# The last query tile of each value burst behind the query-major scores, and no constant matmul ahead of the burst

## The chip, the core and the metric

The kernel runs on one core of one Trainium2 chip. Its engines work side by side and meet at semaphores: TensorE (PE: matmuls, and PEld: weight loads that overlap them), VectorE (DVE), ScalarE (ACT), GpSimd (POOL), and SyncE (SP), which issues DMAs. Matmuls write to PSUM, from which DVE and ACT read. The metric is the device time of one launch in microseconds (us); less is better.

## What is computed

A block of a network, forward and backward: attention over 2048 tokens with 32 heads of width 18, beside a state-space convolution (S4) with a state of 128 in each of 576 channels, mixed by a gate that depends on the token. The outputs are the block's result and the gradients of eleven of its parameters and of its input. The change lies in the attention part alone, whose forward is:

```
scores = jnp.einsum("bhqd,bhkd->bhqk", q, k) * (Dh ** -0.5)
p = _softmax(scores, axis=-1)
o = jnp.einsum("bhqk,bhkd->bhqd", p, v)
```

Its backward needs, for each head, dv = pT dO, ds = p * (dO vT - row sums), dq = ds k and dk = dsT q. The scores are not kept: p is worked out twice, once with the keys along the partitions (for o and ds) and once with the queries along the partitions (for dv).

## The kernel before

**Stages.** A first stage makes q, k, v and the convolution's parameters; the attention stage follows (about 120 to 2090 us of the profiled span), during which POOL also prepares tables for the convolution; the last stage does the convolution, its gradients and the output projections. Only the attention stage is touched.

**Units and steps.** A unit is four heads and 512 queries; there are 8 x 4 = 32 units. The loop at L1289 runs over steps G; each unit has 32 steps. In a step the first pass works on the unit of the moment and the second pass on work that is 39 steps older (OFF, L1118). All five engines run in the order in which the program is written; nothing is rescheduled.

**One step, in the order in which PE gets it:**
1. *P1*: two matmuls of the first pass, queries times keys, into one tile of the PSUM tag "S" (two buffers of two banks). ACT turns it into PT with an exponential of 128x1024 (L1388).
2. *A burst*, by the slot of the step, which is (G - 38) mod 8. Slots 0 and 1: value gradient accV. Slots 2 and 3: query gradient accQ. Slots 5 and 6: key gradient accK. Slots 4 and 7: transposes (turn_p) or the transposes of a finished output. Every burst writes the one buffer of the PSUM tag "accB", and each is read out by DVE before the next may begin.
3. *P3*: two matmuls of the second pass, query-major scores, into the other tile of "S". ACT turns it into eb (L1393).
4. *P2*: two matmuls, dO times vT, each into its own buffer of the tag "dP" (two buffers). DVE multiplies each with a PT tile into ds (L1398).
5. In slots 1, 2, 5 and 6 four matmuls of the output, accO.

In the trace P1 is ps_P<-QaT_g,KaT_g, P3 is ps_P<-KaT_g,QaT_g and P2 is ps_P<-dOaT,VaT_g; all have line L30, a helper's.

**The value burst.** One key block of 512 keys ("a tile" below means the eight steps of one key block; there are 128) has four query tiles ii = 0 to 3, and the eb tiles of query tile ii come from two steps. dv_half (L1136) runs ii = 0 and 1 in slot 0, and ii = 2 and 3 in slot 1, each with four matmuls. The eb of ii = 3 is finished by ACT in the step just before slot 1. In front of slot 0's half stands the constant matmul, fill (L1131): J_bf times the identity into accB, 512 columns wide; its result is overwritten by the burst's first matmul. NFILL (L955) says how many there are.

**The eviction.** At the end of slot 1's half DVE adds accV to a running sum, dvacc (L1146 to L1151). These closures are collected in evs and run ahead of the ACT and DVE work of the step (L1382):

```
for e_ in evs:
    e_()
for (kind, g, b, i, j, ps) in rows:
```

so that on DVE dvacc stands in front of the two ds of its step.

Of the kernel before, what the change touches and what calls it, by code (L numbers as in the profile page):

```python
# [20 lines left out]
def build(tc, aps, dbg_aps=None, stages=("s1", "attn", "post", "s4", "final")):  # L21
# [40 lines left out]
    with ExitStack() as gctx:  # L62
# [66 lines left out]
        with ExitStack() as ctx:  # L129
# [5 lines left out]
            V, AC, GP = nc.vector, nc.scalar, nc.gpsimd  # L135
# [443 lines left out]
        Q = {}  # L579
# [370 lines left out]
        if "attn" in stages:  # L950
# [3 lines left out]
            DA = HP  # L954
            NFILL = {"V": 1, "Q": 0, "K": 0}  # L955
            with ExitStack() as ctx:
# [131 lines left out]
                def by_pe(p):  # L1088

                    return {NPF: 0, NPF + 1: 1}.get(p, 2)  # L1090
# [45 lines left out]
                def dv_half(g, b, kq, h, acc):  # L1136
                    U = UN[(g, b)]
                    for ii in (2 * h, 2 * h + 1):
                        for j in range(4):
                            mm(acc[HP * j:HP * (j + 1), :], lhsT=U["dOa"][:, ii, j, :], rhs=U["eb"].pop((kq, ii, j)),  # L1140
                               start=(ii == 0), stop=(ii == 3), tile_position=(0, HP * j))

                    def ev():
# [145 lines left out]
                for G in range(NTOT + OFF + 24):  # L1289
# [14 lines left out]
                    if 0 <= G2 < NTOT:  # L1304
                        u2, s2 = divmod(G2, NST)
                        r2 = (units[u2][0], units[u2][1], s2)
                    rows = []
                    if r1:
# [5 lines left out]
                        rows.append(("P1", g, b, i, j0, ps))  # L1314
                    evs = []
                    slot = (G2 + 1) % 8
# [7 lines left out]
                    elif 0 <= m_ < NTOT // 8:  # L1324
                        u_, kq = divmod(m_, NQ)
                        g, b = units[u_]
                        if slot in SLOTS:
                            nm, burst, h = SLOTS[slot]
# [17 lines left out]
                    if r2:  # L1346
# [11 lines left out]
                        for x in range(2):  # L1358
                            j2 = 2 * (1 - par_) + x
                            ps = apsp.tile([P, KB], F32, tag="dP", bufs=2, name="ps_P2")  # L1360
                            row(ps, T["VaT", i2 // TPQ][:, (i2 % TPQ) * P:(i2 % TPQ + 1) * P], U["dOaT"].rearrange("p t q -> p (t q)"), j2)
                            rows.append(("P2", g, b, i2, j2, ps))
                    tail = []
                    if G % 8 in (0, 3, 4, 7) and G >= 3:
# [16 lines left out]

                    for e_ in evs:  # L1382
                        e_()
                    for (kind, g, b, i, j, ps) in rows:
# [9 lines left out]
                        else:  # L1394
# [3 lines left out]
                            nc.vector.tensor_tensor(U["ds"][i][:, j, :], ps, U["PT"][i, j // 2][:, j % 2, :], op=A.mult)  # L1398
                            U["dsn", i] += 1
                            nj = 3 if by_pe(i // 2) >= 2 - i % 2 else 4  # L1400
                            if U["dsn", i] == nj:
# [473 lines left out]
```

## Time and profile before

| what | us |
|---|---|
| runs of the kernel | 2666.23, 2686.29, 2685.02 |
| their median | 2685.02 |
| span of the profiled execution (first to last instruction) | 2673.6 |
| mean granted clock of TensorE in it | 0.968 |

The profile gives of the profiled execution its span alone. A row of a table of groups or of the timeline has: start, length, engine, line, operation, out<-in by the program's names, shapes, count, and in brackets the idle time of the engine before it with what ended that. Matmul lengths are modelled and overlap: four matmuls in different quarters of the array run side by side, so that groups follow each other at 0.32 us although each row says 0.39. ACT's and DVE's rows overlap by the tail of the one before. In a table of windows the columns are the stretch, its length, the busy time of PE, PEld, DVE, ACT and POOL with the number of instructions, the granted clock of TensorE (1.00 is full), the share of the DMA engines and GB/s.

### The profile page before, as it was taken

The page shows a single profiled execution, that of the slowest core. Times are in us where ns is not written, and L with a number is a line of the kernel's source. Part 1 is how long each engine was busy: PE and PEld are TensorE (multiplying, and loading weights), DVE is VectorE, ACT ScalarE, POOL GpSimd, SP SyncE. Part 2 cuts the span into 40 slices and gives each one's busy share as a digit, 9 for nine tenths or more (in the row PEclk, how much of TensorE's full clock was granted, in tenths as well). Part 3 has the DMA queues.
Part 4 walks back from the last instruction along what each step waited for, and adds up shares of the span by engine and source line. Part 5 has one row for each costly group of instructions (what it writes and reads, how often), then busy time and mean ns, then how long its engine had stood idle before and what let it go on. Part 6 is the DMA issues. An engine that isn't in the chain of part 4 may idle for free.

```text
span 2673.6 us, 69952 instructions
## 1 busy us (share of the span) xinstructions
PE 2405.5 (90%) x27411; PEld 1134.6 (42%) x27411; DVE 2294.7 (86%) x4090; ACT 2352.0 (88%) x2744; POOL 1830.1 (68%) x2845
## 2 busy tenths in 40 slices
PE   8999999998889898889898999989988699999999
PEld 4433333333333333333333333333232489998756
DVE  5748999999889999889899999999897499999964
ACT  5589999999999999999999999999996489999321
POOL 0388878888888888888878888887931135555431
PEclk9989999999999999999999999999896699999999
DMA  7747889879979978997898899779668979998996
GB/s 232 202 114 152 150 171 177 162 156 181 169 151 172 185 157 163 173 167 152 165 179 157 157 172 169 154 164 181 134 136 174 224 229 262 260 263 250 269 255 136
DMA packets 1155478, 486.63 MB, mean 182 GB/s; under 512 B 1071062, under 2 KB 1108551, under 8 KB 1152843
## 3 DMA queue, kind: packets, MB, share of 16 engines
q1 hardware_dynamic: 1108346, 339.13, 64.3%
q0 software_dynamic: 44784, 137.52, 19.2%
q10 hardware_dynamic: 2016, 5.51, 0.7%
q8 instruction: 214, 3.51, 0.6%
q14 instruction: 118, 0.96, 0.1%
HBM read 146.27 MB, written 93.80 MB: 90 GB/s over the span
## 4 chain that ended last, share of the span: by engine, by line
ACT 39%; PE 28%; DVE 22%; issue 6%; DMA 3%; POOL 2%; SPq 1%; ACTq 0%; DVEq 0%; POOLq 0%
ACT eb L1393 23%; ACT PT L1388 14%; PE ps_P L30 8%; DVE ds L1398 7%; DVE tz L733 3%; DVE wab L753 3%; PE accV L30 2%; PE ps_dx L30 2%; PE turn_p L1097 2%; DVE tz L736 2%; PE accK L30 2%; DVE HG L738 2%; PE yp L30 2%; DVE Rw L758 1%; DVE dvacc L1151 1%
## 5 line engine op out<-in xcount | busy, mean ns | idle before, releaser
L1398 DVE TENSOR_TENSOR ds<-ps_P,PT 128x512 bf16<-128x512 f32 x2048 | 1312.5, 683 | 127.8 <-PE ps_P L30 87.3
L1393 ACT ACTIVATE eb<-ps_P 128x1024 bf16<-128x1024 f32 x1024 | 1095.7, 1070 | 44.3 <-PE ps_P L30 44.2
L1388 ACT ACTIVATE PT<-ps_P 128x1024 bf16<-128x1024 f32 x1024 | 1099.6, 1075 | 11.0 <-PE ps_P L30 9.5
L30 PE MATMUL ps_P<-dOaT,VaT_g 32*128 32x512 bf16 x2048 | 583.1, 390 | 30.8 <-DVE ds L1398 15.4
L506 POOL TENSOR_TENSOR et<-eG,eT 128x448 f32<-128x448 f32 x576 | 542.9, 963 | 10.7
L30 PE MATMUL ps_P<-QaT_g,KaT_g 32*128 32x512 bf16 x2048 | 404.7, 387 | 126.6 <-ACT PT L1388 122.2
L30 PE MATMUL ps_P<-KaT_g,QaT_g 32*128 32x512 bf16 x2048 | 408.9, 392 | 2.0 <-ACT eb L1393 1.4
L506 POOL TENSOR_TENSOR Eo<-et,et 128x448 bf16<-128x448 f32 x288 | 327.2, 1136 | 20.8
L30 PEld LDWEIGHTS <-KaT_g 32*128 32x128 bf16 x2048 | 147.4, 91 | 456.1 <-issue 438.2
L30 PEld LDWEIGHTS <-QaT_g 32*128 32x128 bf16 x2048 | 115.7, 91 | 288.6 <-issue 266.7
L30 PE MATMUL accV<-eb,dOa 128*32 128x512 bf16 x2048 | 185.6, 396 | 26.8 <-ACT eb L1393 26.5
L30 PE MATMUL accO<-PT,Vtok_g 128*32 128x512 bf16 x2048 | 207.9, 395 | 0.1
L30 PE MATMUL accK<-dsT,Qtok_g 128*32 128x256 bf16 x4096 | 165.3, 283 | 21.3 <-DMA dsT<-ds 19.9
L30 PE MATMUL accQ<-ds,Ktok_g 128*32 128x512 bf16 x2048 | 161.9, 394 | 2.2 <-DVE dvacc L1151 1.9
L30 PEld LDWEIGHTS <-Vtok_g 128*32 128x32 bf16 x2048 | 52.8, 93 | 222.6 <-issue 222.6
L1102 DVE COPY dsT<-turn_p 128x1024 bf16<-128x1024 bf16 (+1 forms) x216 | 139.2, 644 | 3.4 <-PE turn_p L1097 3.4
L1097 PE MATMUL turn_p<-ident_bf,ds 128*128 128x128 bf16 x1664 | 136.2, 225 | 1.4 <-DVE gb L1169 0.8
L672 ACT COPY E1e<-etp 128x1024 bf16<-128x1024 bf16 x132 | 125.4, 1063 | 2.7 <-PE etp L671 2.7
L30 PEld LDWEIGHTS <-Qtok_g 128*32 128x32 bf16 x4096 | 88.6, 97 | 87.8 <-issue 57.9
L506 POOL TENSOR_TENSOR et<-eT 128x32 f32<-128x32 f32 (+3 forms) x288 | 116.2, 424 | 11.4
L1097 PEld LDWEIGHTS <-ds 128*128 128x128 bf16 x1664 | 98.9, 100 | 50.2 <-issue 50.0
L1075 POOL COPY dtk<-gT 128x288 bf16<-128x288 bf16 x96 | 40.9, 426 | 107.6 <-DMA dqkv_d<-dtk 47.2
(295 smaller groups left out, 3731.0 us busy)
## 6 DMA issues: line engine op xcount, KB each, us to landing
E_d<-Eo POOLq DMA_DIRECT2D x144, 256.0 KB, 3.3
E1n<-E_d POOLq DMA_DIRECT2D x30, 1024.0 KB, 6.6
T0w<-Kp_d SPq DMA_DIRECT2D x18, 1024.0 KB
xs<-xb_d POOLq DMA_DIRECT2D x28, 512.0 KB, 9.9
dsT<-ds SPq DMA_TRANSPOSE x512
dqkv_d<-dtk POOLq DMA_DIRECT2D x96, 72.0 KB, 4.3
Md_d<-mst SPq DMA_DIRECT2D x18, 288.0 KB
skw<-Md_d SPq DMA_DIRECT2D x72, 64.0 KB
```

What stands on the lines that cost most here:

```text
L30: return nc.tensor.matmul(out, lhsT=lhsT, rhs=rhs, start=start, stop=stop, **kw)
L506: nc.gpsimd.tensor_tensor(out, a, b, op=op)
L672: copy(E_[:, 4 * q:4 * q + 4], pt_)
L733: nc.vector.tensor_tensor(tz[x], HG[:, :, k - 1].unsqueeze(1).to_broadcast([P, 2, 2, n, CB]), ZZ.unsqueeze(3).to_broadcast([P, 2, 2, n, CB ...
L736: nc.vector.tensor_tensor(tz[x][:, 0], tz[x][:, 0], UVk[:, :, :, k, :], op=A.add)
L738: nc.vector.tensor_tensor(HG[:, :, k], tz[x][:, 0], tz[x][:, 1, ::-1], op=A.add)
L753: nc.vector.tensor_tensor(wab, h_, w_, op=A.mult)
L1097: nc.tensor.transpose(pt_[:, x, qb, :], t_[:, qb * P:(qb + 1) * P], ident_bf)
L1102: (nc.scalar.copy if NTOT <= now[0] < NTOT + OFF else nc.vector.tensor_copy)(o_(), pt_[:, x:x + n])
L1388: nc.scalar.activation(U["PT"][i, j // 2], ps, ACT.Exp)
L1393: nc.scalar.activation(e, ps, ACT.Exp)
L1398: nc.vector.tensor_tensor(U["ds"][i][:, j, :], ps, U["PT"][i, j // 2][:, j % 2, :], op=A.mult)
```

## The change

Three things, all in the attention loop.

First, NFILL["V"] is 0: no constant matmul in front of accV. Second, in slot 1 the four matmuls of query tile 3 are not issued with those of tile 2; they are put in a list, late, and issued behind the step's P3 and P2 rows. Third, in those steps the eviction of accV no longer runs ahead of the ds, but between the first and the second ds of the step.

```diff
-            NFILL = {"V": 1, "Q": 0, "K": 0}
+            NFILL = {"V": 0, "Q": 0, "K": 0}
...
-                    for ii in (2 * h, 2 * h + 1):
+
+                    def stored(ii):
                         for j in range(4):
                             mm(acc[HP * j:HP * (j + 1), :], lhsT=U["dOa"][:, ii, j, :], rhs=U["eb"].pop((kq, ii, j)),
                                start=(ii == 0), stop=(ii == 3), tile_position=(0, HP * j))
+                    stored(2 * h)
+                    if h == 0:
+                        stored(1)
+                    else:
+                        late.append(lambda: stored(3))
...
-                    evs = []
+                    evs, late = [], []
...
                             rows.append(("P2", g, b, i2, j2, ps))
+                    for f in late:
+                        f()
                     tail = []
...
-                    for e_ in evs:
-                        e_()
+                    if not (late and r2):
+                        for e_ in evs:
+                            e_()
...
                             U["dsn", i] += 1
+                            if late and r2 and j % 2 == 0:
+                                for e_ in evs:
+                                    e_()
```

What this does to the order of the instructions, on the two engines that meet there. Names are those of the trace; a row's last number is the shape it writes, and "waits" names the semaphores it has to wait for, by engine. Rows that only repeat, and weight loads, are left out at "...".

PE before, from the P1 of slot 0 to the accQ of slot 2:

```order
L30 MATMUL ps_P_5509<-QaT_g,KaT_g 128x512 [waits Activation_49]
...
L30 MATMUL accV<-ident_bf,J_bf 128x512 [waits DVE_49]
...
L30 MATMUL accV<-eb,dOa_1234 32x512
...
L30 MATMUL ps_P_5522<-KaT_g,QaT_g 128x512 [waits Activation_49]
...
L30 MATMUL ps_P_5540<-QaT_g,KaT_g 128x512 [waits Activation_49]
...
L30 MATMUL accV<-eb,dOa_1234 32x512 [waits Activation_49]
...
L30 MATMUL ps_P_5551<-KaT_g,QaT_g 128x512 [waits PE_49]
...
L30 MATMUL ps_P_5554<-dOaT,VaT_g 128x512 [waits DVE_49]
...
L30 MATMUL accO<-PT,Vtok_g 32x512
...
L30 MATMUL ps_P_5575<-QaT_g,KaT_g 128x512 [waits Activation_49]
...
L30 MATMUL accQ<-ds,Ktok_g 32x512 [waits DVE_49]
```

PE now, the same place:

```order
L30 MATMUL ps_P_5497<-QaT_g,KaT_g 128x512 [waits Activation_49]
...
L30 MATMUL accV<-eb,dOa_1234 32x512 [waits DVE_49]
...
L30 MATMUL ps_P_5509<-KaT_g,QaT_g 128x512 [waits Activation_49]
...
L30 MATMUL ps_P_5527<-QaT_g,KaT_g 128x512 [waits Activation_49]
...
L30 MATMUL accV<-eb,dOa_1234 32x512
...
L30 MATMUL ps_P_5534<-KaT_g,QaT_g 128x512 [waits Activation_49]
...
L30 MATMUL ps_P_5537<-dOaT,VaT_g 128x512 [waits DVE_49]
...
L30 MATMUL accV<-eb,dOa_1234 32x512
...
L30 MATMUL accO<-PT,Vtok_g 32x512
...
L30 MATMUL ps_P_5562<-QaT_g,KaT_g 128x512 [waits Activation_49]
...
L30 MATMUL accQ<-ds,Ktok_g 32x512 [waits DVE_49]
```

The constant matmul is gone, and its wait for DVE (for accB) is now on the first accV. In slot 1 the wait for ACT has moved from the fifth accV to P3 (ps_P_5534), and the last accV stand between P2 and accO. The first accQ waits for DVE in both.

DVE before, slots 0 to 2 (two ds each, the eviction dvacc in slot 1, the dqa of slot 3 as the last row):

```order
L1398 TENSOR_TENSOR ds<-ps_P_5525,PT 128x512 [waits PE_49,Activation_49]
L1398 TENSOR_TENSOR ds<-ps_P_5527,PT 128x512 [waits PE_49]
L1151 TENSOR_TENSOR dvacc<-dvacc,accV 128x512 [waits PE_49]
L1398 TENSOR_TENSOR ds<-ps_P_5554,PT 128x512 [waits DMAHW4_49,PE_49,Activation_49]
L1398 TENSOR_TENSOR ds<-ps_P_5556,PT 128x512 [waits PE_49]
L1398 TENSOR_TENSOR ds<-ps_P_5590,PT 128x512 [waits PE_49,Activation_49]
L1398 TENSOR_TENSOR ds<-ps_P_5592,PT 128x512 [waits PE_49]
L1164 TENSOR_SCALAR dqa<-accQ 128x512 [waits DVE_49,PE_49]
```

DVE now:

```order
L1407 TENSOR_TENSOR ds<-ps_P_5512,PT 128x512 [waits PE_49,Activation_49]
L1407 TENSOR_TENSOR ds<-ps_P_5514,PT 128x512 [waits PE_49]
L1407 TENSOR_TENSOR ds<-ps_P_5537,PT 128x512 [waits DMAHW4_49,PE_49,Activation_49]
L1157 TENSOR_TENSOR dvacc<-dvacc,accV 128x512 [waits PE_49]
L1407 TENSOR_TENSOR ds<-ps_P_5539,PT 128x512
L1407 TENSOR_TENSOR ds<-ps_P_5577,PT 128x512 [waits PE_49,Activation_49]
L1407 TENSOR_TENSOR ds<-ps_P_5579,PT 128x512 [waits PE_49]
L1170 TENSOR_SCALAR dqa<-accQ 128x512 [waits DVE_49,PE_49]
```

dvacc has moved behind the first ds of slot 1, ds<-ps_P_5537, which reads the first P2 of that slot. ACT's, POOL's and SP's own instructions keep their order and number.

## The prediction, made before the changed kernel was run

> **What bounds the kernel now.** I read the page first: busy shares, slices, chain.
>
> ```profile
> PE 2405.5 (90%) x27411; PEld 1134.6 (42%) x27411; DVE 2294.7 (86%) x4090; ACT 2352.0 (88%) x2744; POOL 1830.1 (68%) x2845
> ...
> PEclk9989999999999999999999999999896699999999
> ...
> ACT 39%; PE 28%; DVE 22%; issue 6%; DMA 3%; POOL 2%; SPq 1%; ACTq 0%; DVEq 0%; POOLq 0%
> ```
>
> Over the whole span three engines look alike, so the shares decide nothing. The table of windows, asked for the attention stage alone, does: ACT is busy in 1807.93 of 1821.00 us.
>
> ```profile
> 180.00:2001.00 1821.00, 1640.65 (x17627) 570.29 (x17626) 1634.33 (x2692) 1807.93 (x1962) 1512.70 (x2462) 0.99 0.85 163
> ```
>
> Only 13.1 us of idle ACT are left there, and PE and DVE each have over 180 us. The stage lasts as long as ACT's row of exponentials, and any edit is worth what it does to that row. Next the timeline of ACT over one tile, from slot 0 (PT at 1016.16) to slot 2.
>
> ```profile
> 1016.16 1.17 ACT L1388 ACTIVATE PT<-ps_P 128x1024 bf16<-128x1024 f32 x1
> 1017.16 1.08 ACT L1393 ACTIVATE eb<-ps_P 128x1024 bf16<-128x1024 f32 x1
> 1018.08 1.07 ACT L1388 ACTIVATE PT<-ps_P 128x1024 bf16<-128x1024 f32 x1
> 1019.11 1.02 ACT L1393 ACTIVATE eb<-ps_P 128x1024 bf16<-128x1024 f32 x1
> 1020.03 1.02 ACT L1388 ACTIVATE PT<-ps_P 128x1024 bf16<-128x1024 f32 x1
> 1020.94 1.03 ACT L1393 ACTIVATE eb<-ps_P 128x1024 bf16<-128x1024 f32 x1
> ```
>
> Neighbours overlap, so starts mislead; the ends (start plus length) are 1017.33, 1018.24, 1019.15, 1020.13, 1021.05, 1021.97. They are 0.91 to 0.92 apart, but 0.98 at the eb of slot 1. That is what the value burst costs ACT: 0.07 us a tile. Slot 0, where the constant matmul stands, costs it nothing: 0.91. PE and DVE over the same stretch:
>
> ```profile
> 1015.86 0.39 PE L30 MATMUL accV<-ident_bf,J_bf 128*128 128x512 bf16 x1
> 1016.18 0.61 PE L30 MATMUL accV<-eb,dOa 128*32 128x512 bf16 x8
> 1016.73 0.39 PE L30 MATMUL ps_P<-KaT_g,QaT_g 32*128 32x512 bf16 x2
> 1016.74 0.39 PE L30 MATMUL ps_P<-dOaT,VaT_g 32*128 32x512 bf16 x2
> ...
> 1018.29 0.40 PE L30 MATMUL accV<-eb,dOa 128*32 128x512 bf16 x4 [0.20 <-ACT eb L1393]
> 1018.62 0.39 PE L30 MATMUL ps_P<-KaT_g,QaT_g 32*128 32x512 bf16 x2
> 1018.63 0.39 PE L30 MATMUL ps_P<-dOaT,VaT_g 32*128 32x512 bf16 x2
> ...
> 1019.28 0.39 PE L30 MATMUL ps_P<-QaT_g,KaT_g 32*128 32x512 bf16 x2
> 1019.60 0.61 PE L30 MATMUL accQ<-ds,Ktok_g 128*32 128x512 bf16 x8
> 1020.19 0.39 PE L30 MATMUL ps_P<-KaT_g,QaT_g 32*128 32x512 bf16 x2
> ```
> ```profile
> 1017.26 1.29 DVE L1398 TENSOR_TENSOR ds<-ps_P,PT 128x512 bf16<-128x512 f32 x2 [0.66 <-PE ps_P L30]
> 1018.74 0.69 DVE L1151 TENSOR_TENSOR dvacc<-dvacc,accV 128x512 f32<-128x512 f32 x1 [0.18 <-PE accV L30]
> 1019.34 2.67 DVE L1398 TENSOR_TENSOR ds<-ps_P,PT 128x512 bf16<-128x512 f32 x4
> ```
>
> In slot 1 the last four accV matmuls wait for the eb that ends at 1018.24, start 0.05 later, and the P3 rows that feed the next eb stand behind them. The list of waits counts 125 such places:
>
> ```profile
> PE accV L30 <- ACT eb L1393: 26.5, 125, 0.8
> ```
>
> **The change, part by part.**
>
> *The move, its gain.* P3 needs only the buffer that the same eb releases, so it starts at 1018.29 in place of 1018.62. The eb needs it 0.49 earlier than its own start (1018.62 to 1019.11) and is then no longer late. Gain: 0.07 x 125 = 8 us; the other end is 0.
>
> *The move, the new wait.* accB has one buffer. The query burst of slot 2 may write it when DVE has read accV out, and DVE, in its new order, does that behind the first ds of slot 1, which waits for the first P2 row, which stands behind P3. Worked out with the latencies above:
> - P3 at 1018.29, P2 at 1018.30.
> - From P2 to its ds is 0.52 (1016.74 to 1017.26): first ds at 1018.82. DVE is free by then (its ds of slot 0 end at 1018.55).
> - DVE starts its next read 0.61 later (two ds take 1.29, one 0.68): dvacc at 1019.43, 0.69 long, ends 1020.12. It ended at 1019.43 before. Its own input, the moved matmuls behind P2, is long there: P2 at 1018.30 plus 0.32 a group, plus 0.45 from accV to dvacc, is 1019.07.
> - accQ 0.05 later: 1020.17, where it was 1019.60.
> - Eight such matmuls hold PE for 0.55 (1016.18 to 1016.73): P3 of slot 2 at 1020.72.
> - eb 0.49 later at 1021.21, 1.02 long: ends 1022.23. It ended at 1021.97.
>
> So the tile is 0.26 us longer with the gain of slot 1 already in it: without the wait eb would end at 1021.90. Times 125: **+32 us**. Lower end: P3 to eb took 0.43 once (1016.73 to 1017.16), which makes 0.20 and +25. Upper end: if everything that accQ is late, 0.57, reached ACT, less the 0.07, +62; but accQ had 0.2 of slack, so I take the worked-out value, nearer the lower end. Queued behind the waiting accQ on PE are P3, P2 and accO of slot 2; behind dvacc on DVE is the second ds, which ends about 0.1 later than before, and DVE has idle time in the next slots for that. In the order SP and POOL have the same 852 and the same POOL instructions; no DMA is added or moved past another. The transposed loads that read a finished dvacc are issued two steps later and find it done.
>
> *The constant matmul, its gain.* 128 instructions of 0.32 (1015.86 to 1016.18). At most 41 us if PE were the bound; ACT's ends in slot 0 are 0.91 apart, so 0: the matmul lies under the PT of slot 0 that ACT is working on, and PE, done earlier, waits for the S buffer instead. Were that cover gone, the 41 would be the price.
>
> *The constant matmul, its loss.* PE's clock is not constant in this stage. I asked the table of windows for the stretches round the places where it fell; columns are us, then PE, PEld, DVE, ACT, POOL busy, then the granted clock.
>
> ```profile
> 1014.80:1018.20 3.40, 2.74 (x25) 0.71 (x22) 2.74 (x6) 3.40 (x5) 3.02 (x4) 1.00 1.09 184
> 1016.70:1020.10 3.40, 2.96 (x36) 0.83 (x32) 2.65 (x5) 3.40 (x5) 3.08 (x5) 1.00 1.11 225
> 1127.50:1130.90 3.40, 2.50 (x29) 0.86 (x28) 2.87 (x5) 3.40 (x5) 3.00 (x5) 1.00 0.98 99
> 1130.90:1137.70 6.80, 5.69 (x49) 2.07 (x48) 3.85 (x6) 4.05 (x5) 4.35 (x7) 0.50 1.11 199
> 1885.20:1888.70 3.50, 1.97 (x35) 1.07 (x33) 1.71 (x4) 2.99 (x4) 3.42 (x7) 0.99 0.83 110
> 1888.70:1909.10 20.40, 20.23 (x154) 5.67 (x152) 14.28 (x25) 15.88 (x16) 18.76 (x22) 0.50 0.52 116
> 1909.10:1929.60 20.50, 18.36 (x196) 6.03 (x191) 18.14 (x30) 20.11 (x22) 18.46 (x43) 1.00 0.62 150
> 2045.70:2049.10 3.40, 2.33 (x28) 0.78 (x27) 1.78 (x3) 2.94 (x4) 0.89 (x2) 1.00 1.27 211
> 700.80:704.20 3.40, 2.58 (x36) 0.88 (x33) 2.02 (x5) 3.40 (x5) 3.31 (x5) 1.00 0.77 165
> 175.20:202.50 27.30, 25.70 (x181) 6.82 (x177) 18.78 (x30) 23.68 (x26) 25.00 (x50) 0.50 0.54 130
> ```
>
> The clock changes in steps of about 3.4 us (spells of 6.8, 20.4 and 27.3). It fell after a stretch with PE busy for 2.50 of 3.40 us and after one with 1.97; it held through 2.58, and once through 2.33. The emptiest place of a normal tile, slots 7 to 1, has 2.74 with the constant matmul in it. Without it that is 2.42. The stretch with the new wait, 1016.70 on, has 2.96, and loses the 0.5 us of accQ that start 0.57 later: 2.46. Both are below 2.50. A spell is dear: in 20.40 us ACT got 16 instructions through, in the next 20.50 us 22, so it lost 6/22 of 20.4 = 5.6 us. In the same way the 27.3 us spell (26 against 29) lost about 3, the 6.8 us one (5 against 7.3) about 2: mean 3.6, over 18 us. My estimate of how many: each of the two places is low for some 0.4 us of starting points, and a 3.4 us grid that drifts against the tile hits one of them in 0.8/3.4 = 0.23 of 125 tiles, 29; half of these hold, as the rows near 2.5 do: 14, and 12 after leaving out tiles that a spell covers. 12 x 3.6 = **+43 us**. Ends: 0 (all hold), and 25 x 3.6 = 90.
>
> [...]
>
> **The sum.** 32 + 43 = +75 us. The profiled execution's span is 2673.6; the page gives no time around it. The median of the runs, 2685.02, is 11.4 above it, and I carry the difference onto the median: **2760 us**, range of this case 2730 to 2820.
>
> **The rivals.**
> - *The wait alone, the clock holds.* 2685 + 32 = 2717 (2705 to 2735). For it: the 2.33 and 2.58 that held. [...] Against it: 2.42 and 2.46 recurring in every tile.
> - *Not slower.* The wait on accB never reaches ACT and the 8 us remain: 2677. eb is on time if P3 of slot 2 starts by 1020.39 (0.49 before 1021.90 less 1.02), so accQ by 1019.84 and the first ds by 1018.49, 0.19 after its P2 row. It decides at that latency: the rows show 0.52.
> - *PE was the bound in slot 0.* Up to 41 us faster, 2644; ACT's 0.91 there and the 13.1 us of its idle time in all speak against it.
> - *The clock falls in most of the tiles it can.* 32 + 90: 2807. It is the upper end of my case.
> - That the change does not do what it says is ruled out by the order: 128 weight loads and matmuls fewer, four accV matmuls behind P2.
>
> **How the numbers follow.** Clock spells 0.50; wait alone 0.35; not slower 0.12; PE bound 0.03. A measurement of this kernel can tell about 1%, 27 us, from no change: 2658 to 2712. The wait alone lies below 2712 in about a quarter of its cases (0.09), so same is 0.12 + 0.09 = 0.21, faster 0.03, slower 0.76. The range from 2703 to 2815 leaves out the not slower cases and the tails, some 0.2.
>
> **What would show it.** Right: DVE dvacc ends about 1.9 us after the eb of slot 0, in place of 1.2; a new wait PE accQ <- DVE dvacc, some 120 times, about 0.3 us each; PE accV <- ACT eb gone; ACT eb of slot 2 about 0.3 late; the granted clock of the stage below 0.99 with spells at 0.50 spread over it. Wrong: accQ not waiting; eb waits gone everywhere; PEclk as before, which leaves the 32.

## The result, and the profile after

The changed kernel takes 2754.45 us (median of 6 runs, 2748.65 to 2768.57), the kernel before 2681.2 in 6 runs beside it. The ratio is 1.0285, with a 95% interval of 1.0254 to 1.0315: slower, by 73 us. The profiled execution has a span of 2751.2 us, 77.6 more than before's, at a mean granted clock of 0.935 (0.968 before). Of all the executions behind this document one, of the kernel with the half-wide constant matmul below, took 9326 us, and it is left out of that kernel's median.

First the page of the changed kernel: busy time, the slices' clock, the chain by engine and its first lines.

```profile
PE 2439.4 (89%) x27283; PEld 1160.7 (42%) x27283; DVE 2289.1 (83%) x4090; ACT 2367.6 (86%) x2744; POOL 1826.7 (66%) x2845
...
PEclk9989999999999999999999999999996699999999
...
PE 37%; ACT 31%; DVE 21%; issue 6%; DMA 3%; SPq 2%; POOL 0%; ACTq 0%; DVEq 0%; POOLq 0%
ACT eb L1402 20%; PE ps_P L30 13%; ACT PT L1397 9%; PE accQ L30 6%; DVE ds L1407 6%; PE accK L30 3%; PE accO L30 3%; DVE tz L733 2%; DVE wab L753 2%; PE ps_dx L30 2%; DVE dvacc L1157 2%; DVE tz L736 2%; DVE HG L738 1%; PE yp L30 1%; DVE Rw L758 1%
```

The chain has moved from ACT (39% before, 31% now) to PE (28%, now 37%): ACT now waits for matmuls where PE used to wait for ACT. The clock's line hides what matters: a slice is 69 us long, and a spell of a few us doesn't show in its tenths. The window of the attention stage shows it as a mean, 0.95 in place of 0.99, and ACT's busy time there as 1759.50 in place of 1807.93:

```profile
180.00:2001.00 1821.00, 1605.93 (x16878) 568.01 (x16877) 1571.79 (x2598) 1759.50 (x1894) 1486.13 (x2440) 0.95 0.83 158
```

**The wait.** The timeline of the changed kernel over the tile whose rows of before the prediction shows (slot 0 to slot 2), for ACT, then PE from slot 1's P3 on, then DVE from slot 1's first ds on:

```profile
1049.23 1.14 ACT L1397 ACTIVATE PT<-ps_P 128x1024 bf16<-128x1024 f32 x1
1050.14 1.16 ACT L1402 ACTIVATE eb<-ps_P 128x1024 bf16<-128x1024 f32 x1
1051.04 1.17 ACT L1397 ACTIVATE PT<-ps_P 128x1024 bf16<-128x1024 f32 x1
1051.95 1.18 ACT L1402 ACTIVATE eb<-ps_P 128x1024 bf16<-128x1024 f32 x1
1052.85 1.19 ACT L1397 ACTIVATE PT<-ps_P 128x1024 bf16<-128x1024 f32 x1
1054.18 1.02 ACT L1402 ACTIVATE eb<-ps_P 128x1024 bf16<-128x1024 f32 x1
```
```profile
1051.35 0.39 PE L30 MATMUL ps_P<-KaT_g,QaT_g 32*128 32x512 bf16 x2 [0.20 <-ACT eb L1402]
1051.35 0.40 PE L30 MATMUL ps_P<-dOaT,VaT_g 32*128 32x512 bf16 x2
1051.69 0.40 PE L30 MATMUL accV<-eb,dOa 128*32 128x512 bf16 x4
...
1053.20 0.61 PE L30 MATMUL accQ<-ds,Ktok_g 128*32 128x512 bf16 x8 [0.55 <-DVE dvacc L1157]
1053.75 0.39 PE L30 MATMUL ps_P<-KaT_g,QaT_g 32*128 32x512 bf16 x2
```
```profile
1051.86 0.69 DVE L1407 TENSOR_TENSOR ds<-ps_P,PT 128x512 bf16<-128x512 f32 x1 [0.53 <-ACT eb L1402]
1052.47 0.68 DVE L1157 TENSOR_TENSOR dvacc<-dvacc,accV 128x512 f32<-128x512 f32 x1
1053.07 0.69 DVE L1407 TENSOR_TENSOR ds<-ps_P,PT 128x512 bf16<-128x512 f32 x1
```

ACT's ends are 1050.37, 1051.30, 1052.21, 1053.13, 1054.04, 1055.20. The eb of slot 1 is no longer late (0.92 after the end before it, where before had 0.98); the eb of slot 2 is (1.16 in place of 0.92). Backwards from it: P3 of slot 2 stands behind accQ, accQ starts 0.05 us after dvacc has ended (1053.15), and dvacc began only when the first ds of slot 1 let it. PE stood idle for 0.55 us. The list of waits has the new wait 94 times (some matmul records are missing), and the old one once in place of 125 times:

```profile
PE accQ L30 <- DVE dvacc L1157: 40.0, 70, 1.1
...
PE accQ L30 <- DVE dvacc L1152: 13.0, 24, 0.6
...
PE accV L30 <- ACT eb L1402: 0.6, 1, 0.6
```

**The clock.** A fall below is a change of the granted clock from 1.00 to 0.50, and a spell is the time until it is back at 1.00. A stretch is one interval of the grid of 3.41 us on which all changes of the clock in the traces lie (the last section has the evidence); its place is given by the slot in which it begins, 7.2 being a fifth of the way from the PT of slot 7 to the next PT. The table of windows of the changed kernel at two places where the clock fell, the first a stretch that begins in slot 7, the second one that begins in slot 0 and holds the new wait:

```profile
1324.80:1328.20 3.40, 2.47 (x25) 0.83 (x23) 2.85 (x5) 3.40 (x5) 3.17 (x3) 1.00 0.85 183
1328.20:1331.60 3.40, 3.40 (x26) 0.48 (x22) 1.89 (x3) 2.68 (x3) 0.00 (x0) 0.50 1.17 202
1331.60:1335.00 3.40, 2.96 (x31) 1.05 (x28) 3.16 (x6) 3.26 (x4) 0.00 (x0) 1.00 0.25 57
1372.50:1376.00 3.50, 2.38 (x27) 0.84 (x27) 2.81 (x5) 3.50 (x5) 3.37 (x4) 0.99 1.39 196
1376.00:1379.40 3.40, 3.40 (x30) 0.56 (x23) 1.65 (x3) 2.64 (x3) 3.04 (x5) 0.50 0.79 192
```

PE is busy for 2.47 of 3.40 us, and in the next stretch the clock is at 0.50; PE then has no idle time left (3.40 of 3.40), and ACT, which waits for its rows, falls to 2.68. In the third stretch the clock is back.

**The account.** The same reading can be done over the whole stage. From the ACT rows I took the length of each of 122 tiles (end of the eb of slot 7 to the end of the next one) and set apart those that a spell of halved clock touches, or that begin within 2 us behind one. The median of the others is the tile at full clock: 14.728 us before, 14.909 after. So the wait, with the 0.06 us of slot 1 gained, costs 0.181 x 122 = 22 us. The tiles with spells are together 13.9 us longer than so many at full clock before (3 spells, 55 us in all), and 53.0 after (44 spells, 208 us): 39 more. One of these spells, at the start of the stage, is in every kernel of this document. The undisturbed tiles that are longer than the median add 4.5, nearly all of it in tiles that hold the accF transposes, the transposes of a finished output in slot 4. That makes the 65.7 us by which these 122 tiles (186.4 to 1998.9 us before) have grown; the other 12 us of the two spans lie ahead of them (2.8) and behind them (9.1), and there the profiled executions of the kernels below differ by as much without a change in the code (the end takes 674 to 684 us).

### The profile page after: what moved, and what is told of

Its sections match the earlier page's. It is cut to its first block, busy times and chain, and to the rows that moved or that the text cites. A ratio compares the mean times of both kernels' runs of the same rounds, so it can differ in the third digit from the quotient of the medians.

```text
span 2751.2 us, 69696 instructions
## 1 busy us (share of the span) xinstructions
PE 2439.4 (89%) x27283; PEld 1160.7 (42%) x27283; DVE 2289.1 (83%) x4090; ACT 2367.6 (86%) x2744; POOL 1826.7 (66%) x2845
## 4 chain that ended last, share of the span: by engine, by line
PE 37%; ACT 31%; DVE 21%; issue 6%; DMA 3%; SPq 2%; POOL 0%; ACTq 0%; DVEq 0%; POOLq 0%
ACT eb L1402 20%; PE ps_P L30 13%; ACT PT L1397 9%; PE accQ L30 6%; DVE ds L1407 6%; PE accK L30 3%; PE accO L30 3%; DVE tz L733 2%; DVE wab L753 2%; PE ps_dx L30 2%; DVE dvacc L1157 2%; DVE tz L736 2%; DVE HG L738 1%; PE yp L30 1%; DVE Rw L758 1%
## 5 line engine op out<-in xcount | busy, mean ns | idle before, releaser
L30 PE MATMUL ps_P<-dOaT,VaT_g 32*128 32x512 bf16 x2048 | 599.4, 403 | 24.7 <-DVE ds L1407 14.9
L30 PE MATMUL ps_P<-QaT_g,KaT_g 32*128 32x512 bf16 x2048 | 419.4, 396 | 119.6 <-ACT PT L1397 116.1
L30 PE MATMUL ps_P<-KaT_g,QaT_g 32*128 32x512 bf16 x2048 | 424.3, 405 | 25.9 <-ACT eb L1402 24.1
L30 PEld LDWEIGHTS <-QaT_g 32*128 32x128 bf16 x2048 | 130.1, 92 | 334.7 <-issue 311.5
L30 PE MATMUL accQ<-ds,Ktok_g 128*32 128x512 bf16 x2048 | 185.3, 444 | 53.6 <-DVE dvacc L1157 40.0
L30 PE MATMUL accO<-PT,Vtok_g 128*32 128x512 bf16 x2048 | 218.5, 416 | 0.1
L30 PE MATMUL accV<-eb,dOa 128*32 128x512 bf16 x2048 | 193.7, 412 | 2.2 <-ACT dsT L1102 1.5
L1049 POOL TENSOR_TENSOR dOa<-dO_b,rl 128x288 bf16<-128x288 bf16 x32 | 21.5, 673 | 211.5 <-DVE rl L1044 211.5
```

Source lines behind the costliest of these rows:

```text
L30: return nc.tensor.matmul(out, lhsT=lhsT, rhs=rhs, start=start, stop=stop, **kw)
```

## The experiments

All edits are made in the attention loop; times are medians, "above before" is against runs of the kernel before on the same chip in the same round. The constant matmuls added below are overwritten by the matmul that follows, and each kernel computes the whole of the reference.

**The two halves by themselves.** First the changed kernel with the constant matmul back:

```diff
-            NFILL = {"V": 0, "Q": 0, "K": 0}
+            NFILL = {"V": 1, "Q": 0, "K": 0}
```

> The changed kernel with the constant matmul put back; the moved matmuls and the eviction behind the first ds stay. My theory (two causes: the new wait on accB, and clock spells, most of which follow a stretch that begins in slot 7 where the constant matmul is missing, some a stretch that begins at the wait): the wait stays whole, about 70 + 24 us at accQ <- dvacc and the eb of slot 2 about 0.25 us late; the spells after slot 7 go, the dozen after the wait stay. 2681 + 23 + 12 = about 2716 us (2700 to 2735), some 11 spells. Rival, the missing constant matmul is the whole loss: 2681 or less. Rival, the wait is the whole loss and the spells follow from it: about 2754.

Measured: 2741.89 us, 68 above before (ratio 1.0240, 1.0188 to 1.0292). Outside my range: the tile at full clock is 14.907 us, as it should be, and no stretch that begins in slot 7 or 0 lets the clock fall any more, but there are 11 spells, 8 of them at a place where neither kernel had one, and they last long (171 us in all, 46 us of loss). The rival that the missing constant matmul is the whole loss falls. The table of windows at one of the 8, and PE's timeline in that stretch:

```profile
722.50:725.90 3.40, 2.68 (x24) 1.00 (x24) 3.37 (x8) 3.40 (x5) 3.32 (x4) 1.00 0.77 159
725.90:749.80 23.90, 23.72 (x195) 6.73 (x187) 16.76 (x28) 18.81 (x20) 22.24 (x28) 0.50 0.80 151
```
```profile
723.19 0.39 PE L30 MATMUL ps_P<-QaT_g,KaT_g 32*128 32x512 bf16 x2 [0.17 <-ACT PT L1397]
723.85 0.66 PE L1039 MATMUL accF<-ident_f,oT 128*128 128x128 f32 x4 [0.26 <-DVE dqa L1175]
```

The stretch holds the accF transposes of slot 4, which stand in 30 tiles where the others have turn_p. They wait for DVE, and come 0.30 us later in the slot than before (by the median 0.09 us ahead of its PT in place of 0.39). Of the stretches that begin in slots 2.8 to 3.4, 11 have accF in them, and 8 of those fell; of the 29 without, none. (In before 7 with accF, none fell.) The 8 are all those that begin in slots 2.98 to 3.35.

Next the constant matmul taken from the kernel before, and nothing else:

```diff
-            NFILL = {"V": 1, "Q": 0, "K": 0}
+            NFILL = {"V": 0, "Q": 0, "K": 0}
```

> The kernel before with the constant matmul taken out and nothing else changed. My theory: no wait of accQ on dvacc, the eb of slot 1 still 0.06 us late a tile, but some 30 clock spells of about 3.4 us after stretches that begin in slot 7, about 1.1 us each: 2681 + 33 = about 2714 us (2690 to 2730). Rival, the clock falls only because of the new wait: 2681, within 5. Rival, the constant matmul was itself on the path: up to 41 us less, 2640.

Measured: 2718.99 us, 45 above before (1.0172, 1.0132 to 1.0213). The tile at full clock is 14.728 us, to the nanosecond that of before: the constant matmul cost nothing on the path. There are 24 spells where before has 3, fewer than the 30 expected, but they last 9 us on average, not 3.4, and cost 2.3 us each, not 1.1: that the time came out in my range is luck in part. Of the falls 21 follow stretches that begin in slots 6.8 to 7.6, as this one from the table of windows:

```profile
1577.90:1581.30 3.40, 2.54 (x25) 0.75 (x23) 2.86 (x5) 3.40 (x5) 2.95 (x11) 1.00 0.72 193
1581.30:1584.70 3.40, 3.40 (x26) 0.57 (x22) 1.92 (x3) 2.78 (x3) 2.93 (x7) 0.50 0.69 153
```

So either half alone is slow, and they don't add up: 68 and 45 make 73 together. In the changed kernel 32 falls follow stretches that begin in slots 6.8 to 7.6 and 10 the wait, and none the accF stretches, which made the loss of the first run. The changed kernel met none of these: not one stretch at full clock that begins in slots 2.98 to 3.35 has accF in it. The first run above, the two below with the wait filled and the one with the eviction behind the second ds have 8, 7, 4 and 13 such stretches, and the clock fell after every one; before, before without the constant matmul and the run with the eviction first have 7, 6 and 9, and it held after every one.

**How much of a matmul is needed.** The constant matmul of the kernel before, half as wide:

```diff
-                                fill(acc, NFILL[nm])
+                                fill(acc, NFILL[nm], 2)
```

> The kernel before with the constant matmul half as wide (256 of 512 columns), nothing else changed. The run without it was 45 us slower than before, with 24 spells of halved clock in the stage where before has 3, and no other change in the tile (14.73 us in both where the clock is full). My theory now: the clock falls by how little matmul work a fixed stretch of 3.41 us holds, and a weighted count of the matmuls of each stretch, fitted to the six traces so far (87 falls), gives 3.7 falls for half the constant matmul, where the whole one gives 1.9 and none gives 30. So within 10 us of before, 2674 to 2685 us. Rival, any gap there is enough: as without the constant matmul, 45 us more than before, with some 24 spells. Rival, the loss grows in proportion to what is missing: about 22 us more.

Measured: 2679.34 us, 6 above before (1.0014, 0.9991 to 1.0038), no difference that can be told. Its trace is that of one more execution:

> The same kernel as the run with the half-wide constant matmul, once more for its profile. My theory: 2 to 6 spells of halved clock in the attention stage (before 3, without the constant matmul 24), the tile at full clock 14.73 us, 2674 to 2690 us.

Measured: 2675.61 us; 8 spells, 48 us in all, tile 14.728. That is more spells than I expected, and 5 of the falls follow stretches that begin in slot 7.3, where before has none. But they cost little: half a constant matmul keeps the time nearly as well as a whole one, and that any gap is enough, and that the loss is in proportion, both fall.

**Which idle time.** PE filled during the new wait: a constant matmul goes into the buffer of the next P2 row. Once with the first constant matmul back, once without it:

```diff
+                                if nm == "Q" and r2:
+                                    held = apsp.tile([P, KB], F32, tag="dP", bufs=2, name="ps_P2")
+                                    fill(held, 1)
                                 acc = accB("acc" + nm)
...
-                            ps = apsp.tile([P, KB], F32, tag="dP", bufs=2, name="ps_P2")
+                            ps = held if held is not None and x == 0 else apsp.tile([P, KB], F32, tag="dP", bufs=2, name="ps_P2")
```

> The changed kernel with the constant matmul put back and a second constant matmul of the same size ahead of the query burst of slot 2, into the buffer that the next P2 row overwrites: PE works while accQ waits for dvacc, and nothing else moves. My theory: the wait on accB stays with its cost (the eb of slot 2 about 0.2 to 0.25 us late a tile), the clock spells go nearly all (5 or fewer): 2681 + 23 = about 2704 us (2695 to 2715), some 12 us under the run with the first constant matmul alone. Rival, the spells don't follow from PE's idle time there: as that run, about 2716. Rival, the second constant matmul delays PE itself, by up to 0.39 us a tile: 2754.

Measured: 2734.99 us, 61 above before (1.0241, 1.0176 to 1.0306), 20 above the top of my range. The tile stays at 14.908, but 10 spells are left, 7 of them behind the accF stretches, which begin in slot 3 and which this edit doesn't touch. The run cannot be told from the one with the first constant matmul alone.

> The changed kernel, still without the constant matmul ahead of the value burst, with one constant matmul ahead of the query burst of slot 2 in its place. My theory: the tile at full clock stays at 14.91 us; no clock spell follows a stretch that begins in slot 0.2 to 0.4, where the changed kernel has 9; those that begin in slots 6.8 to 7.5 stay, some 25 to 30. With 22 us of wait and the 40 us that the missing constant matmul cost alone: about 62 us above before, 2735 to 2745 us (2725 to 2757). Rival, PE's work during the wait is what decides all spells: they go, and it is about 22 us above before, 2700.

Measured: 2736.45 us, 63 above before (1.0227, 1.0191 to 1.0263), as expected: of the falls after stretches in slots 0.1 to 0.9 (10 in the changed kernel) none is left, 17 after slot 7 are (25 to 30 expected), and 4 have come at the accF stretches. That the wait decides all spells falls with it.

Then the accF stretch itself, in the kernel with the first constant matmul back:

```diff
                         acc = accB("accF")
+                        fill(acc, 1)
```

> The changed kernel with the constant matmul put back, and one more constant matmul ahead of the four accF transposes of slot 4, which run in 30 of the 122 tiles. In the run with the first constant matmul alone all 8 of the falls that followed a stretch from slot 2.8 to 3.4 lay in the 11 such stretches with accF transposes in them, and none in the 29 without. My theory: these falls go, 2 or 3 spells are left as in before, the tile stays at 14.91 us: 22 us of wait, and some 5 in the tiles with accF: about 25 us above before, 2700 (2692 to 2712). Rival, the spells follow from the wait wherever PE idles, not from the thin stretch: as that run, 60 to 68 us above before.

Measured: 2705.66 us, 25 above before (1.0106, 1.0077 to 1.0135), as expected. One spell is left, the one at the stage's start; the window's clock is 1.00:

```profile
180.00:2001.00 1821.00, 1626.81 (x17470) 581.70 (x17470) 1608.74 (x2664) 1796.51 (x1940) 1508.81 (x2461) 1.00 0.86 162
```

Some 30 matmuls of 0.3 us are worth 36 us of time (2741.89 less 2705.66), or 44 by what each is above its own runs of before.

The 25 us are not the wait of slot 2 alone. By the same account as above 22 come from the tile's 14.909, 10 more from the 30 tiles with accF, and 4 from ahead of and behind the tiles, while the spells cost 11 less than in before. The tiles with accF are 15.247 us long at the median, 0.34 more than the others; in before they have 14.733 where the others have 14.728. One of them, ACT from the PT of slot 4 on, then PE:

```profile
1005.32 1.05 ACT L1398 ACTIVATE PT<-ps_P 128x1024 bf16<-128x1024 f32 x1
1006.41 1.02 ACT L1403 ACTIVATE eb<-ps_P 128x1024 bf16<-128x1024 f32 x1
...
1008.23 1.03 ACT L1403 ACTIVATE eb<-ps_P 128x1024 bf16<-128x1024 f32 x1
1009.35 1.02 ACT L1398 ACTIVATE PT<-ps_P 128x1024 bf16<-128x1024 f32 x1
```
```profile
1005.23 0.38 PE L30 MATMUL accF<-ident_bf,J_bf 128*128 128x512 bf16 x1 [0.26 <-DVE dqa L1175]
...
1008.28 0.37 PE L30 MATMUL ps_P<-dOaT,VaT_g 32*128 32x512 bf16 x1 [0.23 <-DVE ds L1408]
```

The eb of slot 4 ends 1.06 us after the row ahead of it and the PT of slot 6 1.11, in place of 0.92 each: behind the wait of slot 2 PE waits for DVE at accF and at the second P2 of slot 5 too. The first run, without this constant matmul, has such tiles of the same length (15.240), so the lateness there belongs to the wait and not to the matmul added.

**The wait.** The eviction moved, in the kernel with the constant matmul back: one ds later, and ahead of both ds as before the change:

```diff
-                            if late and r2 and j % 2 == 0:
+                            if late and r2 and j % 2 == 1:
```

> The changed kernel with the constant matmul put back and the eviction behind the second ds of slot 1 in place of the first: dvacc ends about 0.61 us later, nothing else moves. My theory of the wait (accQ goes 0.05 us after dvacc, and its lateness reaches the eb of slot 2 one for one past its slack): the tile at full clock grows from 14.91 to about 15.5 us, 122 tiles x 0.61 = 74 us more than the run with the eviction behind the first ds, whose median was 68 us above before: about 140 us above before, some 2815 us (2790 to 2840), less if fewer spells. Rival, the tile's length doesn't hang on dvacc (the buffer is free for another reason): as that run, about 2742.

Measured: 2857.18 us, 184 above before (1.0690, 1.0655 to 1.0725). The tile at full clock is 15.505 us, 0.60 longer than with the eviction behind the first ds, for a dvacc that is one ds (0.61) later: the wait reaches ACT one for one. The time is above my range because of the clock: 43 spells, 92 us of loss; 29 falls follow stretches that begin in slots 0.4 to 1.0 and hold the longer wait, 13 the ones in slots 3.0 to 3.4 that hold accF.

```diff
-                    if not (late and r2):
-                        for e_ in evs:
-                            e_()
+                    for e_ in evs:
+                        e_()
...
-                            if late and r2 and j % 2 == 0:
-                                for e_ in evs:
-                                    e_()
```

> The changed kernel with the constant matmul put back and the eviction of the value burst ahead of both ds of slot 1 again, so that the moved matmuls stand alone. My theory: DVE waits for the moved matmuls, which stand behind P2, then evicts, then does the first ds: dvacc ends about 1.5 us after the eb of slot 0 and accQ waits little or not, but both ds of slot 1 come about 0.33 us later, and what waits for the buffer that they free (the P2 rows of slot 2, then accO and P1 of slot 3) too: the PT of slot 3 late by up to 0.27 us a tile in place of the eb of slot 2. 2681 - 8 + 33 = about 2706 us (2685 to 2720), few clock spells. Rival, the wait is simply gone and the gain of 8 us is left: 2673. Rival, the order of the eviction doesn't matter: as the run with the constant matmul back alone, 2716.

Measured: 2732.41 us, 59 above before (1.0232, 1.0184 to 1.0279), outside my range. The clock is as before (2 spells), but the tile is 15.234 us, 0.51 longer than before where I had forecast 0.21. DVE and PE of that kernel, from the eviction on:

```profile
1012.89 0.69 DVE L1157 TENSOR_TENSOR dvacc<-dvacc,accV 128x512 f32<-128x512 f32 x1 [0.81 <-PE accV L30]
1013.50 2.50 DVE L1406 TENSOR_TENSOR ds<-ps_P,PT 128x512 bf16<-128x512 f32 x4
```
```profile
1013.63 0.61 PE L30 MATMUL accQ<-ds,Ktok_g 128*32 128x512 bf16 x8 [0.25 <-DVE dvacc L1157]
...
1014.83 0.37 PE L30 MATMUL ps_P<-dOaT,VaT_g 32*128 32x512 bf16 x1 [0.23 <-DVE ds L1406]
```

DVE waits 0.81 us for the moved matmuls, and everything behind pays: accQ is still late (0.25), and the second P2 of slot 2 waits for the buffer that the delayed second ds frees, so the PT of slot 3 is late too. So the moved matmuls are worse for the tile without the moved eviction (15.234 us) than with it (14.907).

**A version in which ACT doesn't wait.** If the wait can't be shortened, what feeds ACT may be taken from behind it: the first half of the query burst behind the P3 and P2 rows of slot 2.

```diff
+                    for f in behind:
+                        acc = f()
                     tail = []
```

> The changed kernel with the constant matmul put back and the first half of the query burst moved behind the P3 and P2 rows of slot 2, so that nothing that feeds ACT stands behind the wait for dvacc on PE. My theory: the eb of slots 1 and 2 are both on time, the tile at full clock is 14.66 us where before has 14.73, and if the clock falls no more often than before it is 8 us faster than before: about 2666 us (2655 to 2685). Rival, the late burst makes accO and the P1 row of slot 3 late by what it takes on PE (0.55 us, less the 0.3 that PE has in hand there): up to 30 us above before, 2704. Rival, new thin stretches in slots 2 to 4 make the clock fall some ten times, as in the run with the constant matmul alone put back: up to 35 us more.

Measured: 2795.74 us, 122 above before (1.0463, 1.0433 to 1.0493), far outside my range. Both eb are on time, but PE stops one row later, for the second P2:

```profile
1014.84 0.37 PE L30 MATMUL ps_P<-dOaT,VaT_g 32*128 32x512 bf16 x1 [0.23 <-DVE ds L1415]
1015.14 0.61 PE L30 MATMUL accQ<-ds,Ktok_g 128*32 128x512 bf16 x8
1015.59 0.39 PE L30 MATMUL accO<-PT,Vtok_g 128*32 128x512 bf16 x4
1015.91 0.39 PE L30 MATMUL ps_P<-QaT_g,KaT_g 32*128 32x512 bf16 x2
```

The second ds of slot 1, behind dvacc on DVE, frees that buffer too late, and accQ and accO push the P1 of slot 3 out. The tile is 15.117 us: the first rival, at 47 us rather than 30, and 32 spells on top. What this says is the order that DVE should have: both ds, then dvacc; and that accQ must stand behind all that is urgent:

```diff
-                            if late and r2 and j % 2 == 0:
+                            if late and r2 and j % 2 == 1:
...
                                 mm(accO[(g, b)][HP * j:HP * (j + 1), :], ...
+                    for f in behind:
+                        acc = f()
```

with a constant matmul in slot 2, in the place that the burst has left.

> An attempt at a faster one: the changed kernel with the constant matmul put back, the eviction behind the second ds of slot 1, the first half of the query burst behind the P3, P2 and accO groups of slot 2, and a constant matmul in the place in slot 2 that it left. In the run with the query burst behind the rows alone both eb were on time, but the second P2 of slot 2 waited for the second ds of slot 1, and the P1 of slot 3 came 0.44 us too late. My theory: with both ds of slot 1 undelayed the second P2 is on time; dvacc ends 0.78 us after the PT of slot 2 starts, accQ runs from 0.83 to 1.38, and P1 of slot 3 starts at about 1.44 where PT needs it by 1.40: tile at full clock 14.66 to 14.72 us (before 14.73), and without new clock spells 0 to 8 us faster than before, 2666 to 2675 (2655 to 2690). Rival, the stretches that the query burst has left make the clock fall some 30 times, as in the run with the burst behind the rows alone: 40 to 65 us above before.

Measured: 2670.81 us over 12 executions beside 2681.12 of before: ratio 0.9969, 0.9953 to 0.9985. It is the only kernel here that beats the one before, by 0.3%; the medians of before itself in the five rounds lie between 2673.66 and 2681.2 us, so the gain is small beside what it is measured against. Its timeline from slot 0 on, ACT, then PE and DVE in slot 2:

```profile
1021.70 1.19 ACT L1407 ACTIVATE PT<-ps_P 128x1024 bf16<-128x1024 f32 x1
1022.73 1.08 ACT L1412 ACTIVATE eb<-ps_P 128x1024 bf16<-128x1024 f32 x1
1023.65 1.07 ACT L1407 ACTIVATE PT<-ps_P 128x1024 bf16<-128x1024 f32 x1
1024.55 1.09 ACT L1412 ACTIVATE eb<-ps_P 128x1024 bf16<-128x1024 f32 x1
1025.45 1.10 ACT L1407 ACTIVATE PT<-ps_P 128x1024 bf16<-128x1024 f32 x1
1026.37 1.10 ACT L1412 ACTIVATE eb<-ps_P 128x1024 bf16<-128x1024 f32 x1
```
```profile
1026.31 0.62 PE L30 MATMUL accQ<-ds,Ktok_g 128*32 128x512 bf16 x8
1026.86 0.39 PE L30 MATMUL ps_P<-QaT_g,KaT_g 32*128 32x512 bf16 x2
```
```profile
1025.58 0.68 DVE L1157 TENSOR_TENSOR dvacc<-dvacc,accV 128x512 f32<-128x512 f32 x1
```

ACT's ends, 1022.89 to 1027.47, are 0.91 to 0.92 apart throughout. dvacc ends 2.61 us after the PT of slot 1 began (1026.26 less 1023.65), where the changed kernel has 2.11, and accQ still starts only 0.05 us behind it; but nothing that ACT waits for is late by that. The tile is 14.667 us, and 0.061 x 122 = 7 us is the whole gain of the move.

> The run with the query burst behind accO, without the second constant matmul in slot 2; all else as there. That run was 10 us faster than before with 4 clock spells in the stage. My theory: the tile at full clock stays at 14.67 us, but the stretches of 3.41 us that begin in slots 0.4 to 1.0 and that the query burst has left are thin again, and the clock falls after most of them, as it did 31 times in the run with the burst behind the rows alone: 20 to 35 spells and 40 to 70 us above before, about 2725 us (2705 to 2750). Rival, the moved burst alone made the gain and the constant matmul in slot 2 does nothing: 2671, as with it.

Measured: 2675.84 us, 2 below before (0.9989, 0.9966 to 1.0011); 4 spells, tile 14.667. My expectation is wrong and the rival right: with PE's order this way the stretches that the burst left are not thin enough, and one fall in slot 0.4 is all that came there. So the burst's absence is not what made the clock fall 31 times in the run with the burst behind the rows alone; PE's wait for the second P2, which is gone here (P3 and both P2 together), is the cause left, but no run changed it alone. (The count of matmul work in the last section, fitted to other kernels, forecasts 26 falls there and 3 here, where 31 and 3 were seen.) From the tile this kernel gains the same 7 us as the one with the constant matmul; its interval does not tell it from before.

| kernel | above before, us | tile at full clock, us | spells that touch the 122 tiles: number, us | loss in tiles with spells, us | other tiles above the median, us |
|---|---|---|---|---|---|
| before | 0 | 14.728 | 3, 55 | 13.9 | 1.8 |
| the change | 73 | 14.909 | 44, 208 | 53.0 | 6.3 |
| constant matmul back | 68 | 14.907 | 11, 171 | 45.9 | 8.0 |
| before without it | 45 | 14.728 | 24, 215 | 54.5 | 1.1 |
| before, half of it | 6 | 14.728 | 8, 48 | 10.6 | 0.6 |
| wait filled, constant matmul back | 61 | 14.908 | 10, 99 | 31.7 | 8.2 |
| wait filled only | 63 | 14.908 | 23, 130 | 38.4 | 6.4 |
| accF filled, constant matmul back | 25 | 14.909 | 1, 20 | 2.6 | 11.8 |
| eviction behind the second ds | 184 | 15.505 | 43, 331 | 92.3 | 3.8 |
| eviction first | 59 | 15.234 | 2, 34 | 7.1 | 0.4 |
| query burst behind the rows | 122 | 15.117 | 32, 311 | 81.4 | 0.6 |
| query burst behind accO | -10 | 14.667 | 4, 41 | 13.9 | 1.1 |
| the same, slot 2 not filled | -2 | 14.667 | 4, 38 | 12.0 | 2.6 |

The first column is of medians, the others of the one profiled execution. So the columns don't add up exactly: of the first column up to 15 us (in the run with the wait filled and the constant matmul back) are in none of the others.

## Why the prediction held, step by step

*What bounds the kernel*: ACT's row of exponentials in the attention stage. In every run the length of the tiles follows from what happens between the ends of ACT's rows, which at full clock are 0.916 to 0.917 us apart (the two commonest values in the traces) unless a matmul comes late.

*The move's gain, 8 us*: right. The eb of slot 1 had 8.7 us of lateness in the 122 tiles of before and has 0.1 after; the run with the query burst behind accO keeps the gain, 0.061 us a tile, 7 us.

*The new wait, +32 us*: right in mechanism, too large in size for the tile that I worked it out in; there it is 22 (0.181 x 122). The chain came out as worked out: dvacc 1.85 us after the eb of slot 0 (1.88 worked out), accQ 0.05 after it, P3 0.55 after that. The step that was off is the last: I let the eb follow its P3 after 0.49 us, the distance in slot 1 of before, and it takes 0.43 (1053.75 to 1054.18), which I had kept as the lower end at +25. That makes 0.06 of the 0.08 us between the worked-out 0.26 and the measured 0.18 a tile; dvacc ending 0.03 earlier makes the rest. Both distances recur: 0.49 is the median of slot 1 of before, 0.43 that of slot 0 of before and of slot 2 of the changed kernel. What makes the 0.06 between them no run here shows. And a term is missing: I took the lateness for over after slot 2, because DVE has idle time in the next slots. In the 30 tiles with accF it isn't; there the wait costs 0.34 us more, 10 us in the run with accF filled, part of it hidden under spells in the changed kernel. With it the wait comes to 32 us, and that this is the number I wrote is luck.

*The constant matmul's gain, 0*: right, 14.728 us a tile with it and without.

*The constant matmul's loss, +43 us*: right in size, 39 in the profiled execution, and right in place, but made up otherwise. I had 12 spells of 18 us at 3.6 us each; there are 44 of 4.7 us on average at 1.2 us each. I took the spell's length from the three of before, two of which follow long gaps; after one thin stretch most last a single stretch (38 of the 44 last 3.41 us). And I let half of the thin stretches hold, by the mixed rows of before near 2.5 us of PE time; of the 21 stretches that began in slots 7.2 to 7.4 all fell. What I had nearly right is the product, 216 us of spells where the change has added 153, at 0.20 us of loss for each us of spell where it is 0.26. That the errors cancel is luck.

*The sum, +75 us*: 73 by the medians, 77.6 by the two profiled executions. Of the 77.6 the terms I added make 22 and 39, and 16 lie outside what I costed: 4.5 in undisturbed tiles with accF, 2.8 and 9.1 ahead of and behind the tiles, of which I can't say that the change made them. That the sum comes so near is luck in part. And the terms don't belong to the two edits as I had them: with the constant matmul in place the wait alone makes thin stretches at accF, and costs 68.

*The rivals.* The wait alone with a steady clock, 2717, would have been near for this kernel if PE had been kept busy at two places, ahead of accV and ahead of accF: the run with accF filled, 25 above its before, is that case. PE was at work ahead of the falls: in the 122 tiles of the changed kernel the clock fell 43 times after stretches in which PE was busy for 2.3 to 3.1 of 3.4 us.

*What would show it*: dvacc's end, the new wait (94 records of 0.56 us; that is the 0.57 by which accQ was worked out to be late, and not the 0.3 that I put in that list), the wait for eb gone, the eb of slot 2 late by 0.24 (0.3 forecast) and the clock at 0.95 in the stage are all there. The page's line of the clock by itself would have misled: it reads almost as before.

## What to carry to other kernels

Before moving an eviction or a burst past another instruction, list what each engine will then have in front of the work that feeds the bound engine; an accumulator with one buffer tied PE to DVE's order here (accQ started 0.05 us after dvacc had ended), and the cure that worked here was to put the burst behind the urgent rows and let the eviction come later, not to hasten it; it brought 0.3%. A matmul whose result nobody needs can carry its weight (the kernel before without its constant matmul was 45 us slower): read the granted clock in stretches of a few us, not in the page's tenths, before taking one out or opening a gap of half a microsecond that recurs. And the two edits that each opened a gap did not add up (68 and 45 us alone, 73 together), so each has to be run alone before a loss is put down to one of them.

## What the runs showed of the hardware

- Every change of the granted clock in a trace lies on one grid of 3413 ns, to 3 ns from the first to the last (13 traces with 23 to 117 changes each). So the stretch ahead of each fall can be cut out exactly.
- What told best in these traces whether a stretch is followed by a fall is a weighted count of its matmuls, not PE's busy time and no single gap. The first six traces have 88 falls in some 3050 stretches at full clock. The 88 stretches with the least PE busy time hold 47 of the falls, and the 88 with the longest single idle time of PE hold 19; the 88 with the least weighted count of matmuls by kind, with weights fitted to these traces, hold 86. In that fit a constant matmul (`128*128` in the trace's rows) weighs 13 where one of a burst or row (`128*32` or `32*128`) weighs 3 to 7.5. On the seven later traces, to which it was not fitted, it picks out 89 of 108 in the same way (PE's busy time 58). It is worst at the half-wide constant matmul (1 forecast, 7 seen; the fit that the expectation used gave 3.7) and at the eviction behind the second ds (31 forecast, 42 seen). The fit describes; no run here varied the shape of a matmul alone.
- Thin stretches and grid locked in the changed kernel: from 1420.3 to 1635.4 us it has a fall every 30.7 us, eight in all, nine times 3.413 and two tiles of 14.909 plus 0.9: each spell delays the program just enough that the same place of the second next tile meets the grid again. Two neighbours in the table of windows:

```profile
1543.20:1546.60 3.40, 3.40 (x26) 0.49 (x23) 1.89 (x3) 2.71 (x3) 3.06 (x5) 0.50 1.05 137
1573.90:1577.30 3.40, 3.40 (x30) 0.58 (x26) 1.89 (x3) 2.65 (x3) 1.18 (x1) 0.50 0.98 186
```

- A spell's price follows its length: about 0.25 to 0.35 us for each us in the kinds of spell that recur here. After slot 7 a spell of the changed kernel lasts 4.6 us on average and costs 1.15, and one of the kernel before without the constant matmul, at the same place, lasts 8.9 and costs 2.3; after the accF stretches of the run with the constant matmul back it lasts 16.6 and costs 4.7. So the place alone doesn't set the price. Why the clock returns sooner in one case than in another was not tried.
